# Attention and an expanded feed-forward stage in one kernel: the last rows stored tile by tile, zero fillers, pooled V summed on TensorE, weights split two chunks at a time, another order

## The chip, the cores and the metric

The kernel runs on one core of one Trainium2 chip. The metric is device time in microseconds (us), the median of several runs of one launch. The median before is 948.58 us over 3 runs (947.45 to 950.13).

## What is computed

q, k and v are float32, 8 batches x 8 heads x 576 positions x 64. Each head has a pooled attention (q, k and v averaged over groups of 4 positions, full softmax over 144 keys, result repeated 4 times) plus a local attention (keys at a distance below 4). The sum x, 4608 tokens x 512, passes through two matrix products with a rational function between them.

```
q_d, k_d, v_d = means over 4 positions
out_up  = repeat(softmax(q_d k_d^T / 8) v_d, 4)
out_loc = softmax(mask(q k^T / 8, |i - j| < 4)) v
x = (out_up + out_loc) as 4608 x 512
h = x @ w_in                                  # 512 -> 2048
g = (a0 + a1 h + a2 h^2 + a3 h^3) / (1 + |b0||h| + |b1| h^2 + 1e-6)
out = g @ w_out                               # 2048 -> 512
```

The weights come in as 64-bit words, which the kernel turns into float32 on the chip.

## The kernel before, in words

**Blocks and steps.** The tokens are nine blocks of 512: block b < 8 holds the first 512 positions of batch b, block 8 the last 64 positions (`REST`) of all eight batches. For each block 16 steps run, one for each 128 of the 2048 hidden features. A step has an h part (TensorE, `h_part`), a chain of six ScalarE and up to seven VectorE operations (`middle`) that leaves g as a high and a low part, gh and gl, and an o part (TensorE, `o_part`) that accumulates g @ w_out in four PSUM banks, one for each 128 tokens. Products are made of three terms: high by high, low by high, high by low. The 16 h parts of block 0 take whole float32 matmuls (L1073) instead. The last two steps of the last block are halved by tokens: the first covers tiles 0 and 1 for features 14 and 15, the second tiles 2 and 3.

**Attention** for a batch runs in four pairs of heads beside the steps of an earlier block. Batch 0 stands alone at the start; its four pairs are written in `first.0` to `first.3`, and its pooled V is summed over the four positions of a group by two loads and two accumulating GpSimd DMAs into `vf`, two tiles whose sum is made on TensorE: `part_b` in `weighted` (L899) multiplies the pooled weights with each of the two.

**Weights.** `weights` loads a chunk, scales it on ScalarE (L372) and rebuilds its bits on VectorE (L375, L378). `parts` takes the high part (ScalarE cast, L395) and the remainder as low part (VectorE, L398), chunk by chunk, 32 chunks.

**Stores.** `store` copies each finished PSUM bank (ScalarE L1244, or VectorE L1236 for odd tiles of the last block) and stores it: for blocks 0 to 7 one transfer of 128 rows of 2 KB each (L1248). A tile of the last block is 2 batches x 64 positions. There a pair of tiles is waited for, and two transfers of 64 rows x 2 tiles go out, one issued by SP (L1266), one by ScalarE (L1261).

**Order.** All operations are tasks with a cost in a planner (`Plan`), which lists them by urgency, and the table `SHIFT` moves single tasks in urgency. The engines then run in the fixed order that comes out. In the gaps that the planner sees on TensorE before step 0's o part, `warm` puts filler matmuls on the bf16 identity (L1423).

Of the kernel before, what the change touches and what calls it, by code (L numbers as in the profile page):

```python
# [208 lines left out]
def attention_moe(  # L209
# [107 lines left out]
    vf = [put(f"vf{i}", [KC, NPAIR, 2, 2, D], F32, low[0][half + 2 * i].at) for i in range(2)]  # L317
# [24 lines left out]

    add("POOL", 0.6, consts, (), (ident,))
# [13 lines left out]
    def weights(w, f, spot, due=None):  # L357
# [29 lines left out]
        if w and f >= WHOLE:  # L387
# [15 lines left out]


# [471 lines left out]
    def weighted(cs, bk, due):  # L876
# [128 lines left out]
        add("PE", 1.72 if len(cs) == 2 else 1.404, part_b, turn + pooled_v + ready, avb)  # L1005
# [221 lines left out]
    def store(k):  # L1227
        blk = blocks[k]
        due = due_h(blk.first + blk.nstep + 2)
        for sub in range(blk.nsub):  # L1230
# [20 lines left out]
            elif sub % 2:  # L1251
                both = flat(xsf[blk.slot][0].ap)[:, (sub - 1) * DM : (sub + 1) * DM]
                both = both.rearrange("p (b d) -> p b d", d=DM)
                whole = part(hi, None, 4 * (sub - 1) * DM, 8 * DM)
                rows = out.rearrange("(b s) d -> s b d", s=S)
                for i in range(2):
                    b = 2 * (sub - 1) + i
                    src, dst = both[i * REST : (i + 1) * REST], rows[FULL:, b : b + 3 : 2, :]
                    if i:
                        add(  # L1260
                            "ACT", 0.6, lambda src=src, dst=dst: nc.scalar.dma_start(out=dst, in_=src),  # L1261
                            (whole,), (), due=due + 2,
                        )
                    else:
                        add(
                            "SP", ISSUE, lambda src=src, dst=dst: nc.sync.dma_start(out=dst, in_=src),  # L1266
                            (whole,), (), due=due + 2, load=0.8,
                        )
# [10 lines left out]
    for r in range(POOL):  # L1279
        v = vf[r // 2]  # L1280
        if r % 2:
            add(
                "POOL", 0.93, lambda r=r, v=v: nc.gpsimd.dma_start(out=v.ap, in_=vp[0, r], accum_op=ALU.add),
                (v,), (v,), load=2.1, wait=6.4, more=0.0,
            )
        else:
            add("SP", ISSUE, lambda r=r, v=v: nc.sync.dma_start(out=v.ap, in_=vp[0, r]), (), (v,), load=1.7, more=2.1)
# [150 lines left out]
    with tc.manual_schedule(engines={getattr(ET, e) for e in ("PE", "DVE", "Activation", "Pool", "SP")}):  # L1438
# [24 lines left out]
WARM_FROM = 1.75  # L1463
# [20 lines left out]
H_WHOLE = 16  # L1484
POOL_COST = 4.2
# [19 lines left out]
    },  # L1505
# [4 lines left out]
    },  # L1510
# [4 lines left out]
    },  # L1515
# [4 lines left out]
    },  # L1520
# [8 lines left out]
    "load": {  # L1529
        0: -131.9, 2: 38.9, 3: -51.9, 4: -57.2, 5: -8.5, 6: -11.1, 7: -44, 8: -14.4, 9: -99.7, 10: -4.1,  # L1530
        11: -43.1, 12: 1, 13: -76.6,
    },
    "load.0": {
        0: 116.4, 1: 120.8, 2: 15.1, 3: -18.3, 4: 22.1, 5: -20.2, 6: -0.6, 7: -3.8, 8: 1.8, 9: 58.8,
        10: 77.9, 12: 2.9, 13: 11.4, 14: 4.1, 15: 26.4, 16: -32.6, 17: -22.1,
    },
    "load.1": {
        2: -8.9, 3: -0.7, 4: 0.3, 5: 4.8, 6: -32.4, 7: -3.1, 8: 70.8, 9: 10.4, 10: 46.9, 11: -111.9,
        12: 16.3, 13: -21.8, 14: 73.2, 15: -113.5, 16: -30.7, 17: 32.4,
    },  # L1540
    "local.0": {
        0: 23.6, 1: 8.5, 2: 279.5, 3: 745.1, 4: -58.8, 5: -79.6, 6: -80.6, 7: 111, 8: 6, 11: 3.9, 12: 156,
        13: 9.8, 14: 129.7,
    },
    "local.1": {
        0: -22.9, 1: 0.1, 2: 18.3, 3: 607, 4: -2, 5: 1.2, 7: 0.8, 8: -0.5, 9: 465.7, 10: -27.8, 11: -1.3,
        12: 71.5, 13: -5.5, 14: 278,
    },
    "mask": {0: -118.3, 1: -43.7},
    "middle.0": {  # L1550
        0: 10.7, 1: -34.3, 2: 205.9, 3: 4, 4: -0.2, 5: -0.8, 6: -3.4, 7: 91.2, 8: -738.2, 9: 46.5,
        10: 422.1, 11: 27.2, 12: -3.6,
    },
# [37 lines left out]
    "parts": {1: 122.9},  # L1591
# [144 lines left out]
```

## Time and profile before

| what | value |
|---|---|
| median of 3 runs | 948.58 us |
| the profiled execution's own time | 946.54 us |
| its span, first to last instruction | 944.8 us |
| PE (TensorE matmul) busy | 928.8 us, 98% |
| DVE (VectorE) busy | 873.3 us, 92% |
| ACT (ScalarE) busy | 773.6 us, 82% |
| POOL (GpSimd) busy | 148.5 us, 16% |
| instructions | 19636 |

Busy time counts filler matmuls too. The time outside the span is 946.54 - 944.8 = 1.74 us. PEld is TensorE's weight load, SPq and ACTq are the queues that issue transfers.

### The profile page before, as it was taken

To read this page: it belongs to the slowest core of one execution; us is meant where nothing else is said; L and a number is where in the kernel's file an instruction comes from. 1 tells how busy PE (TensorE), PEld (TensorE's weight loads), DVE (VectorE), ACT (ScalarE), POOL (GpSimd) and SP (SyncE) were. 2 spreads that over 40 slices of the span, in tenths; PEclk is the share of its full clock that TensorE was granted. 3 is DMA by queue.
4 is the path that set the end of the run, shared out by engine and by line. 5 is a ranking of instruction groups with operands and counts; after the bars stand their busy time and mean duration, and the time that the engine had idled before them with its cause. 6 is when DMAs were issued, how large, how long until landed. Compare 5 with 4: busy or idle time off the path is not lost.

```text
span 944.8 us, 19636 instructions
## 1 busy us (share of the span) xinstructions
PE 928.8 (98%) x7050; PEld 727.1 (77%) x7050; DVE 873.3 (92%) x1547; ACT 773.6 (82%) x1972; POOL 148.5 (16%) x176
## 2 busy tenths in 40 slices
PE   8999999999999999999999999999999999999996
PEld 7755666788787878787877878787878878887885
DVE  6999999999999999999999999999999988988886
ACT  4899999897897979796979798888988676767674
POOL 1042232130302122221212030304020000000000
PEclk9999999999999999999999999999999999999998
DMA  9697954544565646565657475656633010001001
GB/s 293 261 248 217 275 96 76 180 70 115 93 155 117 132 116 144 146 124 121 130 163 137 110 125 149 117 133 119 172 63 91 1 45 1 1 0 46 1 1 46
DMA packets 93098, 109.34 MB, mean 116 GB/s; under 512 B 23080, under 2 KB 75304, under 8 KB 93000
## 3 DMA queue, kind: packets, MB, share of 16 engines
q1 hardware_dynamic: 69480, 86.90, 30.7%
q0 software_dynamic: 23232, 20.66, 16.4%
q8 instruction: 56, 0.92, 0.4%
q10 hardware_dynamic: 288, 0.52, 0.2%
q14 instruction: 42, 0.34, 0.1%
HBM read 87.05 MB, written 20.99 MB: 114 GB/s over the span
## 4 chain that ended last, share of the span: by engine, by line
PE 60%; DVE 18%; ACT 16%; issue 4%; DMA 2%; DVEq 0%; SPq 0%; ACTq 0%
PE psum L1215 27%; PE psum L1085 26%; ACT m L1098 4%; DVE g L1177 4%; ACT el L625 3%; ACT gb L1098 3%; DVE m L1182 2%; DVE m L1142 2%; DVE m L1191 2%; PE psum L889 2%; DVE m L1147 2%; ACT ep L655 1%; DVE m L1151 1%; DVE xf L952 1%; DVE nm L590 1%
## 5 line engine op out<-in xcount | busy, mean ns | idle before, releaser
L1215 PE MATMUL psum<-wh,g 128*128 128x512 f32 x1152 | 369.9, 398 | 1.6 <-ACT xf L1244 0.9
L1085 PE MATMUL psum<-xs,wh 128*128 128x512 f32 (+1 forms) x1040 | 259.3, 389 | 0.4 <-ACT gb L1098 0.2
L1215 PEld LDWEIGHTS psum<-wh,g 128*128 128x128 f32 x1152 | 213.4, 188 | 58.1 <-DVE g L1177 6.8
L1098 ACT ACTIVATE m<-psum,cf 128x512 f32<-128x512 f32 x288 | 210.7, 739 | 55.3 <-PE psum L1085 43.6
L1085 PEld LDWEIGHTS psum<-xs,wh 128*128 128x128 f32 x1040 | 191.9, 188 | 43.0 <-ACT gb L1098 3.0
L1215 PE MATMUL psum<-wl,g 128*128 128x512 f32 x576 | 224.3, 390 | 0.0
L1177 DVE TENSOR_TENSOR g<-m,m 128x512 fp32r<-128x512 f32 x288 | 194.7, 685 | 30.4 <-ACT m L1098 22.4
L1085 PE MATMUL psum<-xs,wl 128*128 128x512 f32 (+1 forms) x520 | 138.8, 389 | 0.0
L1098 ACT ACTIVATE gb<-m 128x512 f32<-128x512 f32 x144 | 92.0, 639 | 45.4 <-DVE m L1142 39.5
L1215 PEld LDWEIGHTS psum<-wl,g 128*128 128x128 f32 x576 | 108.2, 188 | 21.7
L1098 ACT ACTIVATE gb<-psum,cf 128x512 f32<-128x512 f32 x144 | 113.7, 790 | 5.8 <-PE psum L1215 5.6
L1085 PEld LDWEIGHTS psum<-xs,wl 128*128 128x128 f32 x520 | 96.1, 188 | 20.1
L1142 DVE SCALAR_TENSOR_TENSOR m<-m,cf,m 128x512 f32<-128x512 f32 x144 | 106.8, 742 | 1.9 <-ACT m L1098 1.7
L1151 DVE TENSOR_TENSOR m<-m,gb 128x512 f32<-128x512 f32 x144 | 98.4, 684 | 7.7 <-ACT gb L1098 6.6
L1098 ACT ACTIVATE m<-gb 128x512 f32<-128x512 f32 x144 | 91.7, 637 | 15.2 <-DVE m L1147 14.0
L442 POOL DMA_DIRECT2D vq<-in_vq_dram x60 | 52.4, 944 | 315.1 <-DMA vq<-in_vq_dram 287.4
L1182 DVE SCALAR_TENSOR_TENSOR m<-m,g 128x512 f32<-128x512 f32 x144 | 98.6, 685 | 2.4
L1191 DVE TENSOR_TENSOR m<-m,m 128x512 f32<-128x512 f32 x144 | 98.8, 686 | 1.8
L442 POOL DMA_DIRECT2D pq<-in_qkp_dram x84 | 73.1, 906 | 165.6 <-DMA pq<-in_qkp_dram 150.3
L1147 DVE TENSOR_TENSOR m<-m,m 128x512 f32<-128x512 f32 x144 | 98.1, 682 | 0.3 <-ACT m L1098 0.3
L1098 ACT ACTIVATE m<-psum 128x512 f32<-128x512 f32 x144 | 86.5, 601 | 2.7 <-DVE g L1177 1.8
L625 ACT ACTIVATE el<-el,nm 128x64 f32<-128x64 f32 x240 | 80.8, 353 | 2.3 <-DVE nm L617 2.0
(100 smaller groups left out, 882.8 us busy)
## 6 DMA issues: line engine op xcount, KB each, us to landing
qk<-in_qk_dram SPq DMA_DIRECT2D x32, 590.0 KB, 6.0
pq<-in_qkp_dram POOLq DMA_DIRECT2D x84, 144.0 KB, 3.6
vw<-in_vw_dram SPq DMA_DIRECT2D x32, 320.0 KB, 10.9
out_dram<-xf SPq DMA_DIRECT2D x34, 256.0 KB, 2.4
bounce<-tt SPq DMA_DIRECT2D x96, 80.0 KB, 1.9
eu<-bounce SPq DMA_DIRECT2D x40, 160.0 KB
sl<-in_w_out_dram SPq DMA_DIRECT2D x12, 512.0 KB, 4.3
vq<-in_vq_dram POOLq DMA_DIRECT2D x60, 96.0 KB, 3.6
```

The lines of the kernel that those rows point to most:

```text
L442: lambda d=dst, x=src, r=r: nc.gpsimd.dma_start(out=d.ap, in_=rows(x, r), accum_op=ALU.add),
L625: nc.scalar.activation(out=s.el.ap[:, k, j, :], in_=view[:, j, k, :], func=AF.Exp, bias=nm[:, 5 * j + k : 5 * j + k + 1], scale=scale, acc ...
L889: nc.tensor.matmul(dst, lhsT=c.slot.vw.ap[m : m + D, w, :], rhs=src, start=True, stop=True, skip_group_check=True,)
L1085: nc.tensor.matmul(ph.ap[:, f * t : (f + 1) * t], lhsT=(high, low)[j][0][fc].ap[:, c, :], rhs=blk.x[i].ap[:, c, t0 : t0 + t], start=(part_ ...
L1098: add("ACT", cost, lambda: nc.scalar.activation(out=out_.ap, in_=in_, func=func, **kw), (room_in, cf, *more), (out_,))
L1142: lambda: v.scalar_tensor_tensor(out=tb.ap, in0=tq.ap, scalar=b1, in1=tb.ap, op0=ALU.mult, op1=ALU.add),
L1147: add("DVE", 0.602, lambda: v.tensor_tensor(out=ta.ap, in0=ta.ap, in1=tq.ap, op=ALU.mult), (ta, tq), (ta,))
L1151: add("DVE", 0.602, lambda: v.tensor_tensor(out=ta.ap, in0=ta.ap, in1=u.ap, op=ALU.add), (ta, u), (ta,))
L1177: return v.tensor_tensor(out=out, in0=x, in1=y, op=ALU.mult)
L1182: lambda: v.scalar_tensor_tensor(out=tb.ap, in0=tb.ap, scalar=CONE, in1=gh.ap.bitcast(F32), op0=ALU.add, op1=ALU.mult),
L1191: add("DVE", 0.602, lambda: v.tensor_tensor(out=ta.ap, in0=ta.ap, in1=tb.ap, op=op), (ta, tb), (ta,))
L1215: nc.tensor.matmul(ob[sub].ap, lhsT=g[i].ap[:, g0 : g0 + P], rhs=flat((high, low)[j][1][fc].ap), start=(fc == 0 and m == 0), stop=(fc == N ...
```

## The change

Six things change. The tiles of the last block leave one by one: each is stored from its 128 partitions by one SP transfer whose DRAM side is written as 2 batches x 64 rows x 512. The fillers read a tile of zeros, made by VectorE, in place of the identity, and may start at 1.0 us of the planner's time. Pooled V of batch 0 stays in four tiles, loaded by four SP transfers, and `part_b` makes four terms for each half of the keys. The parts of w_in are taken two chunks at a time, and those of w_out too from chunk 2 on. The table `SHIFT` is replaced, and with it the order on all engines.

```diff
@@ the tiles of the parts @@
-            for f in range(NFC):
-                t = put(f"{name}{w}_{f}", [P, NCC, P], F32R)
...
+            for f in range(0, NFC, 2):
+                t = put(f"{name}{w}_{f}", [P, 2, NCC, P], F32R)
...
-    vf = [put(f"vf{i}", [KC, NPAIR, 2, 2, D], F32, low[0][half + 2 * i].at) for i in range(2)]
+    vf = [put(f"vf{i}", [KC, NPAIR, 2, 2, D], F32, low[0][half + 2 * i].at) for i in range(POOL)]
...
+    plain = put("plain", [P, P], BF16, high[0][0].at)
+    add("DVE", 0.06, lambda: nc.vector.memset(plain.ap, 0.0), (), (plain,), due=-100.0)
@@ parts @@
+        if f >= SINGLE[w]:
+            if f % 2:
+                both_parts(w, f - 1, due)
+            return
...
+    def both_parts(w, f, due):
+        hi, lo, word = (x[w][f // 2] for x in sides)
+        src = word.ap.bitcast(F32)
+        add("ACT", 0.88, lambda: nc.scalar.copy(out=hi.ap, in_=src), (lo,), (hi,), due=due)
+        add(
+            "DVE", 1.133,
+            lambda: nc.vector.tensor_tensor(out=lo.ap, in0=src, in1=hi.ap.bitcast(F32), op=ALU.subtract),
+            (lo, hi), (lo,), due=due,
+        )
@@ weighted @@
-        add("PE", 1.72 if len(cs) == 2 else 1.404, part_b, turn + pooled_v + ready, avb)
+        add("PE", 1.72 if len(cs) == 2 else 2.36, part_b, turn + pooled_v + ready, avb)
@@ store, last block @@
-            elif sub % 2:
-                both = flat(xsf[blk.slot][0].ap)[:, (sub - 1) * DM : (sub + 1) * DM]
-                both = both.rearrange("p (b d) -> p b d", d=DM)
...
-                rows = out.rearrange("(b s) d -> s b d", s=S)
-                for i in range(2):
-                    b = 2 * (sub - 1) + i
-                    src, dst = both[i * REST : (i + 1) * REST], rows[FULL:, b : b + 3 : 2, :]
...
+            else:
+                dst = bass.AP(
+                    tensor=out.tensor, offset=out.offset + (2 * sub * S + FULL) * DM,
+                    ap=[[S * DM, 2], [DM, REST], [1, DM]],
+                )
+                add(
+                    "SP", ISSUE, lambda osb=osb, dst=dst: nc.sync.dma_start(out=dst, in_=osb),
+                    (room,), (), due=due + 2, load=0.8,
+                )
@@ pooled V of batch 0 @@
-    for r in range(POOL):
-        v = vf[r // 2]
-        if r % 2:
-            add(
-                "POOL", 0.93, lambda r=r, v=v: nc.gpsimd.dma_start(out=v.ap, in_=vp[0, r], accum_op=ALU.add),
...
+    for r, v in enumerate(vf):
+        add("SP", ISSUE, lambda r=r, v=v: nc.sync.dma_start(out=v.ap, in_=vp[0, r]), (), (v,), load=1.5)
@@ fillers @@
-                banks[7].ap[:, FULL - P :], lhsT=identb.ap, rhs=identb.ap,
+                banks[7].ap[:, FULL - P :], lhsT=plain.ap, rhs=plain.ap,
...
-WARM_FROM = 1.75
+WARM_FROM = 1.0
+SINGLE = (0, 2)
...
-    "alone.0": {0: -77.2, 2: 1.5, 3: -118.1, 4: -6.9},
+    "alone.0": {0: -64.9, 1: -24.7, 3: -21.5, 4: -80},
```

The order at three places. First SP's queue at its end, before; the tiles of the last block lie in xf_0 side by side, and the shape is that of the DRAM side:

```order
L745 DMA bounce_p<-tp_201 32x5x80
L745 DMA bounce<-tt_193 32x4x160
L745 DMA eq_200<-bounce_p 64x3x144 x2
L745 DMA eu_198<-bounce 64x2x320 x2
L1248 DMA out_dram<-xf_0_154 128x512 x4
L1248 DMA out_dram<-xf_0_158 128x512 x4
L1266 DMA out_dram<-xf_0_154 64x2x512 x2
```

and in the change:

```order
L766 DMA bounce_p<-tp_153 32x5x64
L766 DMA eu_150<-bounce 64x2x320 x2
L766 DMA eq_152<-bounce_p 64x3x144
L1269 DMA out_dram<-xf_0_106 128x512 x4
L1269 DMA out_dram<-xf_0_110 128x512 x4
L1278 DMA out_dram<-xf_0_106 2x64x512 x4
```

Two transfers of 64x2x512 on SP (and the two like them at the end of ACT's queue) become four of 2x64x512, all on SP.

Second, PE's last rows, before; g_168 and g_170 are gh and gl of the first half step (tiles 0 and 1), g_167 and g_169 those of the second (tiles 2 and 3), wh and wl the parts of w_out:

```order
L1215 MATMUL psum<-wl_15_150,g_168 128x512
L1215 MATMUL psum<-wh_14_86,g_167 128x512 x2
L1215 MATMUL psum<-wh_15_87,g_167 128x512 x2
L1215 MATMUL psum<-wl_14_148,g_167 128x512 x2
L1215 MATMUL psum<-wl_15_150,g_167 128x512 x2
L1215 MATMUL psum<-wh_14_86,g_170 128x512 x2
L1215 MATMUL psum<-wh_15_87,g_170 128x512 x2
L1215 MATMUL psum<-wh_14_86,g_169 128x512
L1215 MATMUL psum<-wh_15_87,g_169 128x512
L1215 MATMUL psum<-wh_14_86,g_169 128x512
L1215 MATMUL psum<-wh_15_87,g_169 128x512
```

and in the change, where one tile holds two chunks of weights, g_120 and g_122 are gh and gl of the first half step, g_119 and g_121 those of the second:

```order
L1236 MATMUL psum<-wl_14_102,g_120 128x512
L1236 MATMUL psum<-wh_14_71,g_120 128x512
L1236 MATMUL psum<-wl_14_102,g_120 128x512
L1236 MATMUL psum<-wh_14_71,g_122 128x512 x4
L1236 MATMUL psum<-wh_14_71,g_119 128x512 x4
L1236 MATMUL psum<-wl_14_102,g_119 128x512 x4
L1236 MATMUL psum<-wh_14_71,g_121 128x512 x4
```

The four matmuls on gl of the first half step, which finish tiles 0 and 1, have moved ahead of the second half step's twelve.

Third, PE in batch 0's attention, from where the second pair's part_b begins, before (ept: pooled weights, et: local weights, vf and vw: values):

```order
L710 MATMUL psum<-ident,el_222 128x128 x4
L899 MATMUL psum<-ept_206,vf_239 64x144 x2
L899 MATMUL psum<-ept_206,vf_240 64x144 x2
L899 MATMUL psum<-ept_206,vf_239 64x144 x2
L899 MATMUL psum<-ept_206,vf_240 64x144 x2
L889 MATMUL psum<-et_208,vw_205 64x58 x2
L889 MATMUL psum<-et_208,vw_205 64x54 x2
L889 MATMUL psum<-et_208,vw_205 64x58 x16
```

and in the change:

```order
L731 MATMUL psum<-ident,el_174 128x128 x4
L920 MATMUL psum<-ept_158,vf_191 64x144 x2
L920 MATMUL psum<-ept_158,vf_192 64x144 x2
L920 MATMUL psum<-ept_158,vf_193 64x144 x2
L920 MATMUL psum<-ept_158,vf_194 64x144 x2
L920 MATMUL psum<-ept_158,vf_191 64x144 x2
L920 MATMUL psum<-ept_158,vf_192 64x144 x2
L920 MATMUL psum<-ept_158,vf_193 64x144 x2
L920 MATMUL psum<-ept_158,vf_194 64x144 x2
L910 MATMUL psum<-et_160,vw_157 64x58 x2
L910 MATMUL psum<-et_160,vw_157 64x54 x2
L582 MATMUL psum<-pq_181 64x144 x6
```

Eight matmuls on pooled V become sixteen for each pair. Over the whole attention of batch 0 the fillers fall from 170 to 131.

## Rows read from the trace of the kernel before

**Rows 1.** The page, part 1: engine, busy us (share of the span), instructions.
```profile
PE 928.8 (98%) x7050; PEld 727.1 (77%) x7050; DVE 873.3 (92%) x1547; ACT 773.6 (82%) x1972; POOL 148.5 (16%) x176
```
**Rows 2.** Busy time by stretch: length, then busy us by engine, granted clock, DMA share, GB/s.
```profile
20.00:30.00 10.00, 9.43 (x177) 8.15 (x175) 7.27 (x20) 9.73 (x47) 0.00 (x0) 1.00 1.03 375
...
80.00:90.00 10.00, 8.40 (x38) 5.36 (x37) 10.00 (x21) 10.00 (x28) 3.30 (x4) 1.00 0.94 267
...
500.00:600.00 100.00, 99.79 (x805) 79.82 (x804) 95.80 (x172) 84.85 (x233) 20.95 (x24) 1.00 0.59 131
...
900.00:945.00 45.00, 37.60 (x187) 31.30 (x185) 32.73 (x51) 24.89 (x40) 0.00 (x0) 0.94 0.08 24
```
**Rows 3.** The chain that ended last, 880 to 945 us: start us, length us, what.
```profile
907.90 2.72 PE psum L1215 x12
...
933.92 4.00 PE psum L1215 x16
```
**Rows 4.** Timeline of the end, by engine: start us, length us, instruction, count.
```profile
935.87 2.03 PE L1215 MATMUL psum<-wh,g 128*128 128x512 f32 x8
936.75 1.31 ACT L1244 COPY xf<-psum 128x512 f32<-128x512 f32 x2 [3.61 <-PE psum L1215]
937.75 1.59 ACTq L1261 DMA_DIRECT2D out_dram<-xf  x2
937.94 0.69 DVE L1236 COPY xf<-psum 128x512 f32<-128x512 f32 x1 [0.27 <-PE psum L1215]
```
**Rows 5.** Transfers, 937 to 945 us: busy tenths in 40 slices; queue: packets, MB, share.
```profile
DMA  0000000000298998989999989998451000000000
...
q10 hardware_dynamic: 288, 0.52, 24.2%
q1 hardware_dynamic: 288, 0.52, 20.6%
```
**Rows 6.** Transfers, 860.5 to 863 us, one store alone.
```profile
GB/s 0 0 0 0 0 0 0 0 0 0 0 0 0 0 0 0 0 0 197 229 360 426 426 360 393 393 426 295 393 230 66 0 0 0 0 0 0 0 0 0
DMA packets 144, 0.26 MB, mean 105 GB/s; under 512 B 16, under 2 KB 16, under 8 KB 144
...
q1 hardware_dynamic: 144, 0.26, 27.9%
```
**Rows 7.** Transfers, 132 to 135 us, two loads of pooled V, 72 rows each.
```profile
q1 hardware_dynamic: 168, 0.15, 17.2%
...
vp<-in_vp_dram SPq DMA_DIRECT2D x2, 72.0 KB
```
**Rows 8.** Groups by line and shape: count, busy us, mean ns, idle before.
```profile
L899 PE MATMUL psum<-ept,vf 72*64 72x144 f32 x64 | 5.0, 294 | 0.0
L1423 PE MATMUL psum<-identb 128*128 128x128 bf16 x170 | 12.3, 235 | 1.6 <-DVE identb L346 1.6
L398 DVE TENSOR_TENSOR wl<-wb,wh 128x512 fp32r<-128x512 f32 x32 | 21.4, 676 | 0.0
L395 ACT CAST wh<-wb 128x512 fp32r<-128x512 f32 x32 | 19.8, 653 | 0.0
L731 ACT COPY et<-psum 128x128 f32<-128x128 f32 x4 | 1.1, 270 | 0.0
```
**Rows 9.** Timeline of PE, 28 to 56 us.
```profile
33.24 1.20 PE L899 MATMUL psum<-ept,vf 72*64 72x144 f32 x16
34.37 1.38 PE L889 MATMUL psum<-et,vw 64*64 64x58 f32 x40
...
43.25 12.28 PE L1073 MATMUL psum<-xf,wb 128*128 128x512 f32 x28
```
**Rows 10.** ACT's exponentials of the last pair, 28 to 32 us.
```profile
L625 ACT ACTIVATE el<-psum,nm 128x64 f32<-128x64 f32 x10 | 3.0, 318 | 0.2 <-DVE nm L617 0.2
```
**Rows 11.** PE's waits, 43 to 165 us: total us, times, longest.
```profile
PE psum L1073 <- ACT gb L1098: 2.0, 2, 1.6
PE psum L528 <- ACT el L625: 1.4, 1, 1.4
```

More of the change, by code (lines that the diff above doesn't have):

```diff
@@ L256, in flat @@
         return t.rearrange("p a b -> p (a b)")
-    high, low, bits = [], [], [[], []]
+    high, low, bits = ([[], []] for _ in range(3))
+    sides = {id(x): [[], []] for x in (high, low, bits)}
     for name, parts in (("wh", high), ("wl", low)):
         for w in range(2):
-            parts.append([])
-            for f in range(NFC):
-                t = put(f"{name}{w}_{f}", [P, NCC, P], F32R)
-                parts[w].append(t)
+            for f in range(0, NFC, 2):
+                t = put(f"{name}{w}_{f}", [P, 2, NCC, P], F32R)
+                both = [(parts, t)]
                 if parts is low:
-                    bits[w].append(put(f"wb{w}_{f}", [P, NCC, P], I32, t.at))
+                    both.append((bits, put(f"wb{w}_{f}", [P, 2, NCC, P], I32, t.at)))
+                for to, x in both:
+                    sides[id(to)][w].append(x)
+                    for i in range(2):
+                        to[w].append(part(x, x.ap[:, i], i * 4 * NCC * P, 4 * NCC * P))
+    sides = [sides[id(x)] for x in (high, low, bits)]
     xs, xsf = [], []
@@ L386, in weights @@
         add("DVE", 0.6, lower, (spot, lo), (lo,))
-        if w and f >= WHOLE:
+        if w:
             parts(w, f)
     def parts(w, f, due=None):
+        if f >= SINGLE[w]:
+            if f % 2:
+                both_parts(w, f - 1, due)
+            return
         hi, lo, word = high[w][f], low[w][f], bits[w][f]
@@ L1250, in store @@
                 )
-            elif sub % 2:
-                both = flat(xsf[blk.slot][0].ap)[:, (sub - 1) * DM : (sub + 1) * DM]
-                both = both.rearrange("p (b d) -> p b d", d=DM)
-                whole = part(hi, None, 4 * (sub - 1) * DM, 8 * DM)
-                rows = out.rearrange("(b s) d -> s b d", s=S)
-                for i in range(2):
-                    b = 2 * (sub - 1) + i
-                    src, dst = both[i * REST : (i + 1) * REST], rows[FULL:, b : b + 3 : 2, :]
-                    if i:
-                        add(
[L1261 to L1268, printed above, removed]
+            else:
[7 more added lines that the diff above has]
+                )
     order = sorted(((w, f) for w in range(2) for f in range(NFC)), key=lambda c: c[1] / 2 + 1.5 * c[0])
@@ L1278, in attention_moe @@
         load_qk(c)
-    for r in range(POOL):
-        v = vf[r // 2]
-        if r % 2:
-            add(
-                "POOL", 0.93, lambda r=r, v=v: nc.gpsimd.dma_start(out=v.ap, in_=vp[0, r], accum_op=ALU.add),
[L1284 to L1287, printed above, removed]
+    for r, v in enumerate(vf):
+        add("SP", ISSUE, lambda r=r, v=v: nc.sync.dma_start(out=v.ap, in_=vp[0, r]), (), (v,), load=1.5)
     for c in c0:
@@ L1536 @@
     },
     "load.1": {
-        2: -8.9, 3: -0.7, 4: 0.3, 5: 4.8, 6: -32.4, 7: -3.1, 8: 70.8, 9: 10.4, 10: 46.9, 11: -111.9,
-        12: 16.3, 13: -21.8, 14: 73.2, 15: -113.5, 16: -30.7, 17: 32.4,
+        0: 198.5, 1: 7.7, 2: 5.9, 3: -1.4, 4: 109.9, 6: 19.3, 7: -46.6, 8: 18.4, 9: -9.6, 11: -8.4, 12: 4.8,
+        13: -4.9, 14: 18.4, 16: -10.1, 17: -15.3,
     },
     "local.0": {
-        0: 23.6, 1: 8.5, 2: 279.5, 3: 745.1, 4: -58.8, 5: -79.6, 6: -80.6, 7: 111, 8: 6, 11: 3.9, 12: 156,
-        13: 9.8, 14: 129.7,
+        0: -46.2, 2: 874.5, 3: 1185.3, 4: -32.4, 5: -29.9, 6: -61.3, 7: 42.5, 8: 6.2, 10: 113.1, 11: 7.3,
@@ L1544 @@
+        12: 25.5, 13: 10.6, 14: 180.1,
     },
     "local.1": {
-        0: -22.9, 1: 0.1, 2: 18.3, 3: 607, 4: -2, 5: 1.2, 7: 0.8, 8: -0.5, 9: 465.7, 10: -27.8, 11: -1.3,
-        12: 71.5, 13: -5.5, 14: 278,
+        0: -59, 1: 22.8, 2: 461.6, 3: 651.1, 4: 4.1, 5: -44.7, 6: 1.6, 7: 96.9, 8: -20.6, 9: 317.9, 10: 17,
+        11: 8.9, 13: 57, 14: 172.8,
     },
-    "mask": {0: -118.3, 1: -43.7},
+    "mask": {0: -10.8, 1: 69.9},
     "middle.0": {
-        0: 10.7, 1: -34.3, 2: 205.9, 3: 4, 4: -0.2, 5: -0.8, 6: -3.4, 7: 91.2, 8: -738.2, 9: 46.5,
-        10: 422.1, 11: 27.2, 12: -3.6,
+        0: -3.5, 1: -128, 2: 64.4, 4: -18.9, 5: -40.1, 6: 31.7, 8: -1089.9, 9: -52.9, 10: 74.4, 11: -28.2,
+        12: -118.9,
@@ L1560 @@
+        12: -15.8,
     },
     "middle.3": {
-        0: 7.5, 1: -124.4, 2: -0.7, 3: -24.3, 4: -281.9, 5: 348.1, 6: 1.3, 7: 81.7, 8: 59.2, 9: -89.8,
-        10: -75.7, 11: 1.4, 12: 130,
+        0: -189.2, 1: -235.8, 3: -30.3, 4: -181.3, 6: -36, 7: -13, 8: 72.1, 9: -180.5, 10: 82.3, 11: -8.8,
+        12: 36.4,
     },
     "middle.4": {
-        0: -5.2, 1: 297.3, 2: 16.9, 4: -278.5, 5: -4.9, 6: -7.6, 7: -32.6, 8: -68, 9: 61.8, 10: -8.9,
-        11: -17.9, 12: -2.1,
+        0: -85.9, 1: -20.4, 2: -7.3, 3: -183.1, 4: -134, 5: 451.6, 7: -44.3, 8: -169.3, 9: 18.9, 10: 1.8,
@@ L1568 @@
+        11: -84.2, 12: 250.5,
     },
     "middle.5": {
-        0: -1.6, 1: -12.8, 2: 31.8, 3: -115.2, 4: -2.7, 5: 2.1, 6: 20, 7: -142.6, 8: 78.1, 9: -14.7,
-        10: -28.9, 11: -1.8, 12: 356.5,
+        0: 78.8, 1: 9.1, 2: 8.2, 3: -156.4, 4: -118.7, 5: 267.8, 6: -22.9, 7: -85.4, 8: 130, 10: 0.2,
+        11: 2.7, 12: 3.1,
     },
     "middle.6": {
-        0: 33.8, 1: -0.2, 2: 123.1, 3: 307.2, 4: 123.1, 5: -48, 6: -56, 7: -18.3, 8: 261.3, 9: -10.2,
-        11: 108.9, 12: 565.7,
+        0: 3.8, 1: -25, 2: 16.2, 3: 368.3, 4: 4.5, 5: -66.9, 6: -61.4, 7: -10.6, 8: 401.5, 9: 8.8,
@@ L1576 @@
+        11: 201.6, 12: 539,
     },
     "middle.7": {
-        0: 191.4, 1: 167.4, 2: 16.9, 3: 286.5, 4: -27.9, 5: 274.9, 6: 599.9, 8: -1.6, 9: -19.9, 10: 76.4,
-        11: 306.3, 12: 206.3,
-    },
[10 rows of a table removed]
-    "parts": {1: 122.9},
[10 rows of a table removed]
+        0: 393.6, 1: 156.6, 2: 87.8, 3: 605.3, 4: 19.5, 5: 429.2, 6: 807.8, 7: 9.9, 8: 48.6, 9: -46.7,
+        10: 183.8, 11: 287.9, 12: 169.5,
+    },
[10 rows of a table added]
+    "parts": {0: 4.1, 1: 227.2},
[9 rows of a table added]
     },
     "quad.1.1": {
[7 rows of a table removed]
[6 rows of a table added]
     },
     "quad.2.0": {
[8 rows of a table removed]
[8 rows of a table added]
     },
     "quad.2.1": {
[7 rows of a table removed]
-    },
@@ L1644 @@
     },
     "turned.1": {
[3 rows of a table removed]
-    },
[10 rows of a table removed]
+        0: 48.8, 1: 304.6, 2: 21.7, 3: 36.9, 4: -10.5, 5: -71.5, 6: 32.1, 7: 128.3, 8: -15.9, 10: 38.4,
+        12: 53.2, 13: -41.9, 14: -1.7, 15: 33.2, 16: 14.5, 18: 56.6, 20: -3.3, 21: 585.1, 22: 8.3, 26: 1,
+        27: -7.9,
+    },
[10 rows of a table added]
 }
```

19 lines of the change are left out of this document (9 added, 10 removed), and 162 rows, old and new, of the table SHIFT.

## The prediction

> **What bounds the kernel now.** I read first the share of each engine over the span, then the busy time stretch by stretch, then the chain that ended last, and at the two ends of the kernel the timeline and the transfers. TensorE is busy 98% of the span [rows 1]. By stretches the reader sees three parts. In the long middle TensorE has hardly a gap: 99.79 of 100 us between 500 and 600 [rows 2]. The number of its matmuls there doesn't change, so a new order can take away a few tenths of a us at most. In the first 160 us it does wait, 8.40 of 10 us busy at the worst [rows 2]. At the end only 37.60 of the last 45 us are busy [rows 2]: the last matmul ends at 935.87 + 2.03 = 937.90 [rows 4], and 944.8 - 937.9 = 6.9 us of the span remain for two copies and the stores. The chain at the end is TensorE's alone, 2.72 us for 12 matmuls, 0.227 us each, until the last 16, which begin late [rows 3]. So three things can move the total: when TensorE's dense run begins, the stalls up to 160 us, and the tail. The sum is made against the profiled execution, whose own 946.54 us lie 2.04 below the median of the three runs, 948.58; I add the differences to the median. A measurement of this kernel can tell about 0.3%, 2.85 us, from no change.
>
> **The tail, which decides.** Before, the four stores go out together. The transfer engines are busy from about 938.8 to 943.3 [rows 5], 1.1 us after the first issue at 937.75 [rows 4], and the span ends 1.5 us after the last byte. One store of 256 KB on its own leaves 144 packets, of which 16 are under 512 B [rows 6]: 128 rows of 2 KB, and 16 small ones. I read the small ones as one for each of the 16 engines used. Two of the last stores (64 rows outermost, 2 tiles inside) leave 288 packets on each queue, 256 of data and again 16 each [rows 5]. Two loads of pooled V, 72 rows outermost, leave 168, that is 144 and only 12 each [rows 7]. So a transfer isn't always dealt over 16 engines: 128 and 64 rows give 16, 72 rows give 12, each time the largest number up to 16 that divides the outermost count. In all of these both sides have the same outermost count. The new store doesn't: 128 partitions on one side, 2 batches x 64 rows on the other. Either the smaller side decides and two engines carry everything, or the SBUF side does and sixteen do. I take two, as a transfer has to be cut at the same places on both sides.
>
> By the Trainium skill, DMA: Bandwidth & Descriptors, section "Why a DMA increments its semaphore by 16 and not by 1", the number of engines is the largest up to 16 that divides the slowest dimension of both patterns; the trace agrees for 72 rows, and no run here shows two sides that differ. By that rule the stores take what I work out next for two engines; by the rows alone both readings below stand.
>
> The price: one store keeps 27.9% of 16 engines busy for 2.5 us [rows 6], 11.2 engine-us, and on two engines that is 5.6 us. If all four use the same two, 22.3 us. Bounds: at the best rate seen, 426 GB/s over 16 engines [rows 6], two move 53 GB/s, and 1.05 MB take 19.7 us. At what the four stores cost when they ran together, (24.2 + 20.6)% of 16 engines over 8 us = 57.3 engine-us [rows 5], they take 28.7 us. I take 22.3, since two engines press on memory no more than the lone store did.
>
> The start of the stores moves ahead. The four matmuls that finish tiles 0 and 1 now stand before the last twelve; tile 0's last one has 13 behind it, so its copy can begin 13 x 0.227 = 2.95 us before TensorE's end, takes 1.31 / 2 = 0.66 [rows 4], and its bytes flow about 1.1 us after the issue: 1.2 us before TensorE's end, where they now begin 0.9 after it. Then 22.3 us and the 1.5 us at the close: 22.6 us behind TensorE's end instead of 6.9, **+15.7 us** (+13.1 to +22.1 by the bounds). SP's queue holds nothing else there, so issuing costs nothing; ScalarE loses two issues that no one waited behind.
>
> TensorE's own end stays. VectorE's copy of tile 1, 0.69 us, now stands ahead of the last two operations on gl, which the last four matmuls wait for. That can cost some 0.4 us, about what is saved from the late start of the last 16 matmuls, which took 4.00 us where 16 x 0.227 = 3.63 would do [rows 3]. Net nothing.
>
> **The start.** Pooled V as four terms doubles the 64 matmul records of L899 [rows 8]. One pair's 16 step on in 34.37 - 33.24 = 1.13 us [rows 9], so +4.5 us of TensorE work for four pairs. The 39 fillers fewer are 39 x 12.3 / 170 = 2.8 us less [rows 8], but a filler lies in a gap and its loss brings nothing forward. From the second pair's part_b at 33.24 to the run of step matmuls at 43.25 [rows 9] TensorE is nearly full, so three pairs' terms, +3.4 us, lie on the path there unless that stretch begins earlier. It can: the order lets ScalarE make the second pair's transposed weights ahead of the last pair's ten exponentials, 3.0 us [rows 10]. I take +0.4 for the start, between -1 (the chain through ScalarE gives more than it costs) and +3.4. Without the two accumulating GpSimd transfers the first pair is ready no later, but nothing waits for the first pair. Four loads in place of two on SP stand among weight loads, 576 KB more ahead of some of them; what covers that is that the first step's matmuls can't run before all four pairs are done.
>
> **Weights by two chunks.** 17 instructions stand for 32 on ScalarE (0.653 us each) and on VectorE (0.676) [rows 8]. 512 columns take 0.653 and 128 take 0.270 [rows 8], so 0.14 us of each is fixed, and 15 x 0.14 = 2.1 us fall away on ScalarE; I take the same for VectorE, as an estimate. The bounds are nothing and 15 whole instructions. Both engines are full at 80 to 90 us [rows 2], and TensorE waited 2.0 + 1.4 us for ScalarE until 165 us [rows 11], so a gain can be had, up to 3.4 us; but a chunk is then ready only with its partner. I take -0.4. Fillers on zeros and their earlier start: the granted clock is 1.00 at 20 to 30 us [rows 2] and the step matmuls keep TensorE dense from 43 us, so nothing.
>
> **Sum**: 15.7 + 0.4 - 0.4 = +15.7. The profiled execution comes to 962.2, the median to **964.3 us**.
>
> **The rivals.** (1) *The SBUF side decides and sixteen engines carry each store.* For it: the 128 rows are on the side that TensorE's results lie in, and the trace has no pair of unequal sides. Against it: the 12 of 72. Then the last tile's copy ends 0.73 us behind TensorE's end [rows 4], its bytes begin 1.1 later, take 0.83 (13 slices of 2.5 / 40 us) [rows 6], and 1.5 us close: 4.2 in place of 6.9, so 945.9 us. That isn't slower; with the start's and the stalls' -1 and -3.4 it is faster, with the start's +3.4 it is the same. The point from which it decides: eight engines or more for a store. The Trainium skill, DMA: Bandwidth & Descriptors, "Rules for kernel authors", advises one 128-partition transfer in place of two over halves, which taken alone speaks for this rival; no run here compares the two. (2) *The start costs what its terms cost*: +3.4 in place of 0.4, with two engines 967.3. For it: the nearly full 10 us before 43.25. Against it: the exponentials moved behind. (3) *The clock falls in the start*, with 39 fillers fewer and their operands zero. The dense 10 us before 43.25 would at worst take 20: 974. Against it: the granted clock was 1.00, its 2.4 GHz level, at 20 to 30 us and at 80 to 90 us, gaps of 1.6 us among them [rows 2, 11]. (4) *The new order brings nothing that can be seen*: this is in the forecast already, as the middle has no gap to give.
>
> **How the numbers follow.** Two engines, the forecast: 0.83; of that (2) has 0.2. Rival (1): 0.13, half of it faster by over 0.3%, half within. Rival (3): 0.02. Otherwise: 0.02. Slower by over 0.3%: 0.83 + 0.02 + 0.01 = 0.86; within 0.06; faster 0.08. The range goes from the fastest price of the stores with the stalls gone, 948.58 + 13.1 - 3.4 = 958.3, to the dearest with the dearer start, 948.58 + 22.1 + 3.4 = 974.1. It leaves out rival (1) and some 0.05 more.
>
> **What would show it.** Right: after the last matmul some 22 us in which only the transfer queue of SP works, at about 50 GB/s and a share of transfer engines near 2/16; 520 packets or so for the last four stores, 8 of them small (two for each store) if two engines are used. Wrong: 16 small packets for each store and an end 4 to 5 us after TensorE's. The start is right if the first long run of step matmuls begins at 42 to 47 us; the weights by two if an instruction on 1024 columns takes about 1.17 us on ScalarE. The forecast as a whole is wrong if the tail behind the last matmul is under 15 us.

## The result, and the profile after

The changed kernel takes **960.94 us** (median of 6 runs, 958.73 to 964.63) against 949.06 for the kernel before on the same chip (6 runs, 947.45 to 951.38): a ratio of 1.0128, 95% interval 1.0101 to 1.0154. That is slower, by 11.9 us. The forecast was 964.3, with 958.3 to 974.1 around it. The profiled execution took 959.22 us; its span is 957.4, 12.6 more than the 944.8 before. Three executions in the experiments below, of 1147.92, 2350.43 and 5228.38 us, were slow as a whole, and no ratio counts them.

Busy time of the engines first, the page's part 1 after the change (it answers to [rows 1]).

```profile
PE 928.6 (97%) x7075; PEld 728.7 (76%) x7075; DVE 872.7 (91%) x1533; ACT 771.8 (81%) x1957; POOL 147.7 (15%) x174
```

TensorE has as much work as before, 928.6 against 928.8 us. So the 12.6 us are time in which it stands still. Busy time by stretch tells where (after; the columns are those of [rows 2]).

```profile
40.00:100.00 60.00, 56.35 (x374) 33.14 (x372) 57.34 (x106) 54.66 (x138) 15.85 (x18) 1.00 0.83 239
...
60.00:70.00 10.00, 7.87 (x70) 5.31 (x69) 8.98 (x16) 8.34 (x22) 5.90 (x7) 1.00 0.83 225
100.00:120.00 20.00, 20.00 (x230) 12.94 (x229) 20.00 (x38) 20.00 (x64) 6.19 (x7) 1.00 0.82 239
500.00:600.00 100.00, 99.98 (x808) 80.38 (x807) 96.21 (x175) 85.42 (x236) 20.78 (x25) 1.00 0.60 133
100.00:930.00 830.00, 829.87 (x6061) 661.53 (x6060) 778.40 (x1355) 687.74 (x1714) 131.16 (x151) 1.00 0.43 99
900.00:945.00 45.00, 35.73 (x178) 29.62 (x176) 31.95 (x48) 23.47 (x38) 0.00 (x0) 0.95 0.03 11
```

Four of these stretches of the kernel before, which its rows above don't have:

```profile
40.00:100.00 60.00, 58.02 (x430) 34.73 (x429) 59.83 (x118) 58.34 (x150) 15.84 (x18) 1.00 0.86 238
...
60.00:70.00 10.00, 9.98 (x116) 6.50 (x117) 10.00 (x19) 9.76 (x33) 6.80 (x8) 1.00 0.88 157
100.00:120.00 20.00, 18.59 (x167) 12.09 (x166) 18.93 (x38) 18.76 (x66) 5.09 (x6) 1.00 0.94 284
100.00:930.00 830.00, 826.46 (x5978) 657.21 (x5977) 776.76 (x1359) 685.05 (x1717) 130.12 (x150) 1.00 0.44 100
```

From 100 to 930 us TensorE stood 3.54 us before and 0.13 now, a gain of 3.4, of which 20.00 - 18.59 = 1.4 lies between 100 and 120 us. From 40 to 100 us it is the other way round, 3.65 us of standing in place of 1.98, most of it at 60 to 70. The rest of the story is the tail. The timeline of the end, after:

```profile
932.57 0.57 ACT L1265 COPY xf<-psum 128x512 f32<-128x512 f32 x1
933.16 9.61 SPq L1278 DMA_DIRECT2D out_dram<-xf  x4
934.14 0.68 DVE L1257 COPY xf<-psum 128x512 f32<-128x512 f32 x1
936.29 1.15 PE L1236 MATMUL psum<-wh,g 128*128 128x512 f32 x4 [0.64 <-DVE g L1198]
937.03 0.59 ACT L1265 COPY xf<-psum 128x512 f32<-128x512 f32 x1 [3.89 <-PE psum L1236]
937.48 0.69 DVE L1257 COPY xf<-psum 128x512 f32<-128x512 f32 x1 [1.33 <-PE psum L1236]
```

The last matmul ends at 936.29 + 1.15 = 937.44 (before 937.90 [rows 4]). 957.4 - 937.44 = 20.0 us of the span remain behind it, where 6.9 remained. What fills them is in the transfers from 930 to 958 us (slices of 0.7 us):

```profile
DMA  0000001011111111111111111111111111111000
GB/s 0 0 0 0 0 0 23 29 23 35 44 50 53 53 50 50 53 53 47 53 53 53 47 53 53 50 50 53 53 50 50 53 53 50 50 53 53 12 0 0
DMA packets 520, 1.05 MB, mean 37 GB/s; under 512 B 8, under 2 KB 8, under 8 KB 520
...
q1 hardware_dynamic: 520, 1.05, 10.2%
```

and in two stretches of the same time:

```profile
934.20:936.30 2.10, 1.46 (x8) 0.91 (x6) 1.91 (x4) 0.00 (x0) 0.00 (x0) 1.00 0.12 25
...
940.00:950.00 10.00, 0.00 (x0) 0.00 (x0) 0.00 (x0) 0.00 (x0) 0.00 (x0) 0.51 0.13 51
```

Bytes flow from about 934.2 to 956, 21.8 us, at 23 to 44 GB/s in the first 3.5 us and at 47 to 53 behind them; before, the four stores were through in 4.5 us [rows 5]. The 8 small packets are two for each store, where a store of 128 rows had 16 [rows 6], and the transfer engines' share is 0.13, two of 16 (0.125): two engines carry everything.

### The profile page after: what moved, and what is told of

Same layout as the page of the kernel before. It is cut to its first block, busy times and chain, and to the rows that moved or that the text cites. A ratio compares the mean times of both kernels' runs of the same rounds, so it can differ in the third digit from the quotient of the medians.

```text
span 957.4 us, 19630 instructions
## 1 busy us (share of the span) xinstructions
PE 928.6 (97%) x7075; PEld 728.7 (76%) x7075; DVE 872.7 (91%) x1533; ACT 771.8 (81%) x1957; POOL 147.7 (15%) x174
## 4 chain that ended last, share of the span: by engine, by line
PE 86%; DVE 5%; DMA 3%; ACT 3%; issue 1%; SPq 0%; DVEq 0%; ACTq 0%
PE psum L1236 39%; PE psum L1106 35%; PE psum L1094 4%; DMA st<-in_w_in_dram 2%; PE psum L910 2%; PE psum L502 1%; PE psum L582 1%; DVE g L1198 1%; ACT m L1119 1%; PE psum L948 1%; PE psum L920 1%; DVE m L1163 1%; ACT gb L1119 1%; DMA sl<-in_w_in_dram 1%; ACT el L646 1%
```

## The experiments

The times before in these runs lie at 946.85, 947.05 and 947.21 us, so each version is compared by its ratio to the kernel before, measured beside it. The ratio is taken over all runs of both; that of the two medians can differ from it by up to 0.0008, or 0.8 us. In the cuts of the edits, `...` stands for lines left out.

**Only the change's store undone.** Does the rest of the change cost anything?

```diff
-                dst = bass.AP(tensor=out.tensor, offset=..., ap=[[S * DM, 2], [DM, REST], [1, DM]])
...
+            elif sub % 2:
...
+                rows = out.rearrange("(b s) d -> s b d", s=S)
+                src, dst = both[i * REST : (i + 1) * REST], rows[FULL:, b : b + 3 : 2, :]
```

> The change with only its last store put back (four transfers of 64x2x512, two on SP and two on ACT, each behind both tiles of its pair); the orders of VectorE, GpSimd and TensorE stay as in the change but for one neighbouring pair of matmuls. Theory (the store is the whole loss, the rest of the change is worth half a us): TensorE's last matmul ends at about 937.4 and the tail is 6.9 us again, so a span near 944.3 and a median near 948.5 us, between 0.5 below and 0.5 above before. Rival (the start or the clock carries part of the loss): 951 us or more. Rival (the new order brought the 3.4 us that it saved between 100 and 900 us, and its losses at 40 to 100 us and at the end belong to the store's order): 946 us or less.

Measured: 947.08 us (12 runs), ratio 0.9996, 0.9978 to 1.0014. The transfers of the end, 930 to 945 us, have their 64 small packets back:

```profile
DMA packets 576, 1.05 MB, mean 70 GB/s; under 512 B 64, under 2 KB 64, under 8 KB 576
```

The whole loss is the store's. All the rest together, the new order with it, comes to nothing that can be told. The rival by which the gain of 3.4 us should show falls too: the profile of this version has the gain (829.79 of 830 us busy from 100 to 930) and the loss of 60 to 70 us (8.03 of 10). Its tail is 5.6 us, not the 6.9 expected, as the new order finishes the first pair of tiles earlier and that pair leaves at 935.7. TensorE's end, 937.13 + 1.16 = 938.3, is 0.9 us later than expected; 0.7 of that is standing in the first 100 us that the change doesn't have.

**The store alone, in the kernel before.** Same queues, same places in every order, same bytes. On the DRAM side the outermost index is the batch (2) in place of the row (64); with it, each transfer takes one tile from 128 partitions in place of two tiles from 64.

```diff
-                rows = out.rearrange("(b s) d -> s b d", s=S)
+                rows = out.rearrange("(b s) d -> b s d", s=S)
...
-                    src, dst = both[i * REST : (i + 1) * REST], rows[FULL:, b : b + 3 : 2, :]
+                    src, dst = both[:, i * DM : (i + 1) * DM], rows[b : b + 2, FULL:, :]
```

> The kernel before with nothing changed but the index that is outermost in its last four stores: 2x64x512 (one tile each) in place of 64x2x512, on the same queues, two on SP and two on ACT, at the same places of every engine's order. Theory (the smaller outermost count sets the number of engines, the same two for both queues): the bytes begin at about 938.8, take the 21.8 us that they took in the change, and 1.5 us close: a span of 962.1, 17.3 us longer, near 966.3 us; 8 small packets among 520, some 50 GB/s. Rival (each queue has engines of its own, so that two pairs of engines share the bytes): 938.8 + 10.9 + 1.5 = 951.2, near 955.5 us. Rival (one queue that issues four transfers behind each other is what is slow, not the shape): as before, 949 us.

Measured: 964.28 us (4 runs), ratio 1.0179, 1.0149 to 1.0208; span 962.3 where 962.1 was expected. The transfers, 930 to 965 us:

```profile
DMA packets 521, 1.06 MB, mean 30 GB/s; under 512 B 8, under 2 KB 8, under 8 KB 520
...
q1 hardware_dynamic: 260, 0.52, 4.4%
q10 hardware_dynamic: 260, 0.52, 3.8%
```

Writing the batch outermost costs 17.4 us by itself (964.28 - 946.85). The stores of the change start earlier, tile by tile; that gives part of it back, 12.5 us being left by the two ratios, (1.0128 - 0.9996) x 949.

**Two queues.** Here the stores of the change alternate between SP and ACT.

```diff
+                if sub % 2:
+                    add("ACT", 0.6, lambda osb=osb, dst=dst: nc.scalar.dma_start(out=dst, in_=osb), ...)
```

> The change with the stores of tiles 1 and 3 issued by ACT and those of tiles 0 and 2 by SP, all still 2x64x512. Theory (the same two engines serve both queues): no change, 960 to 961 us, 50 GB/s in all. Rival (another queue uses another two engines): two tiles on each pair of engines, tile 1's bytes from 936.0 and tile 3's behind them to 946.8, a span of 948.3 and about 951.8 us, at 100 GB/s.

Measured: 962.29 us (4 runs), ratio 1.0157, 1.0125 to 1.0188, with 49 to 52 GB/s in all once the first 2.6 us are over, and 8 small packets. Ten us of it:

```profile
940.00:950.00 10.00, 0.16 (x1) 0.00 (x0) 0.69 (x1) 0.33 (x1) 0.00 (x0) 0.66 0.13 51
```

The share is 0.13 as with one queue, so two engines are at work and not four: the same two serve both queues, and one queue's issuing isn't what is slow.

**Halves.** Each tile goes out as two transfers of 64 rows, so that both sides have 64 outermost.

```diff
-                    ap=[[S * DM, 2], [DM, REST], [1, DM]],
...
+                    for i in range(2):
...
+                            ap=[[DM, REST], [1, DM]],
...
+                        nc.sync.dma_start(out=dst, in_=osb[i * REST : (i + 1) * REST])
```

> The change with each tile's store as two transfers of 64 rows, both on SP at the place of the one, so that both sides have 64 rows outermost; all other orders word for word those of the change. Theory (outermost count): 16 small packets for each transfer, 128 in all, the last tile's copy ends at 938.2, issue and first byte 1.1 us, the bytes under 1 us, 1.5 us to close: a span near 941.7, near 945.2 us, 15.7 us below the change. Rival (one SP queue with stores behind each other is the bound): still near 960 us. Rival (64 partitions reach only half of the engines): a tail of some 6 us, near 947 us.

Measured: 946.57 us (12 runs), ratio 0.9989, 0.9976 to 1.0002, which is 13.2 us below the change by the two ratios, (1.0128 - 0.9989) x 949; 15.7 had been expected. The transfers, 930 to 965 us:

```profile
DMA packets 640, 1.05 MB, mean 30 GB/s; under 512 B 128, under 2 KB 128, under 8 KB 640
```

16 small ones for each of the 8 transfers: sixteen engines again. The tail was 5.5 us in the profile, 1.3 more than expected: the last two tiles follow each other on SP as four issues, and their bytes flow at only some 200 GB/s. TensorE's end lay at 939.1 in that profile, 1.7 us later than in the change, where the same 7075 matmuls were busy 930.7 us in place of 928.6: a dip of the granted clock, which the last section gives. Leaving tile by tile isn't worth measurably more than leaving by pairs (0.9989 against 0.9996, the intervals overlap).

**62 and 2 rows.** Is it the disagreement of the two sides, or the number?

```diff
-                    for i in range(2):
+                    for i, r, n in ((0, 0, 62), (0, 62, 2), (1, 0, 62), (1, 62, 2)):
```

> The halves version with each transfer of 64 rows cut into one of 62 rows and one of 2. Theory (the number of engines is the largest up to 16 that divides the outermost count): 62 rows go to two engines, as in the change, though both sides agree: some 4 small packets for a pair of cuts, 32 in all, 50 GB/s, about 22 us of bytes, near 961 us. Rival (only the two sides' disagreement, or a count under 16, keeps a transfer from sixteen engines): 62 rows spread over about sixteen, at most 2 us more than the halves version, under 949 us.

Measured: 960.76 us (one run). The transfers, 930 to 960 us:

```profile
DMA packets 544, 1.05 MB, mean 35 GB/s; under 512 B 32, under 2 KB 32, under 8 KB 544
```

544 - 32 = 512 rows and 32 small packets, two for each of 16 transfers. Both sides agree on 62 rows, and still two engines carry them, since 2 is the largest number up to 16 that divides 62. So the number decides, as with the 72 rows of [rows 7].

**Both queues, and tile 1 copied by ScalarE.** What hangs on VectorE at the very end?

```diff
-            if k == len(blocks) - 1 and sub % 2:
+            if k == len(blocks) - 1 and sub == 3:
...
+                    if i:
+                        add("ACT", 0.6, lambda src=src, dst=dst: nc.scalar.dma_start(out=dst, in_=src), ...)
```

> The halves version (two transfers of 64 rows for each tile) with two things more: of each tile's two transfers one goes out on SP and one on ACT, and tile 1 is copied by ScalarE, so that VectorE's copy of 0.68 us no longer stands ahead of the last gl; VectorE's and TensorE's order is otherwise that of the change but for one neighbouring pair of matmuls. Theory (TensorE's last stalls hang on VectorE's chain to gl, and the last two tiles' four issues on SP pass the bytes on at only 200 GB/s): the last matmul ends 0.65 us earlier than with that copy (a last stall of 0.64 gone or the one before it shorter), the last bytes leave 0.7 us sooner, 1.3 us in all: near 945.2 us. Rival (the stall hangs on ScalarE, or the four transfers' bytes are the bound): 946.6 us, as the halves version.

Measured: 946.18 us (11 runs), ratio 0.9985, 0.9976 to 0.9995. TensorE's last two stalls, in this version's timeline:

```profile
934.01 1.21 PE L1236 MATMUL psum<-wh,g 128*128 128x512 f32 x4 [0.93 <-DVE g L1198]
...
936.35 1.17 PE L1236 MATMUL psum<-wh,g 128*128 128x512 f32 x4 [0.20 <-DVE g L1198]
```

In the halves version they are

```profile
935.22 1.20 PE L1236 MATMUL psum<-wh,g 128*128 128x512 f32 x4 [1.09 <-DVE g L1198]
...
937.96 1.16 PE L1236 MATMUL psum<-wh,g 128*128 128x512 f32 x4 [0.64 <-DVE g L1198]
```

so the copy cost 1.73 - 1.13 = 0.60 us there, and the tail behind the last matmul is 942.4 - 937.5 = 4.9 in place of 5.5 us. In the profiles the expected 1.3 us are nearly there (0.60 + 0.6). The ratios differ by 0.0004 alone, which is inside their intervals, so the medians don't show them. This version is faster than the kernel before by 0.15%, under the 0.3% of the prediction's bound though its interval leaves out 1, and faster than the change by 1.4%.

**Two of the four terms of pooled V.** The halves version with half of the sum left out of TensorE's work.

```diff
-                terms = [(v, kc) for kc in range(2) for v in vp_of(c)]
+                terms = [(v, kc) for kc in range(2) for v in vp_of(c)[:2]]
```

> The halves version with two of the four terms of pooled V of batch 0 left out of TensorE's work (half of that sum is missing; the four loads stay): TensorE issues 16 matmuls fewer in each pair's record group, 1.05 us a pair, 4.2 us in all. Theory (what the terms cost at the start is mostly hidden, because the waits for ScalarE at 52 to 72 us come next): the first long run of step matmuls begins 1 to 3 us earlier, the waits between 50 and 75 us grow by nearly as much, and the time falls by under 1 us: near 946.0. Rival (the start costs what its terms cost, rival 2 of the prediction): three pairs' terms, 3.2 us, reach the end: 943.4 us.

Measured: 944.91 us (12 runs), ratio 0.9972, 0.9960 to 0.9985: 1.6 us below the halves version (0.0017 x 947), between the two expectations (946.0 and 943.4). The two intervals overlap, so the runs don't decide between them. Its profiled execution, 946.05 us, doesn't show the start at its best. Busy time of 2 us stretches there:

```profile
20.00:22.00 2.00, 0.66 (x12) 0.49 (x9) 1.99 (x5) 2.00 (x16) 0.00 (x0) 1.00 0.99 232
22.00:24.00 2.00, 1.51 (x38) 1.48 (x39) 1.66 (x5) 2.00 (x14) 0.00 (x0) 0.94 1.04 301
24.00:26.00 2.00, 2.00 (x19) 1.80 (x18) 1.90 (x6) 2.00 (x8) 0.00 (x0) 0.50 1.01 382
26.00:28.00 2.00, 2.00 (x21) 1.49 (x20) 0.61 (x1) 0.03 (x1) 0.00 (x0) 0.50 1.03 392
28.00:30.00 2.00, 2.00 (x15) 1.97 (x14) 1.56 (x5) 1.29 (x4) 0.00 (x0) 0.50 1.00 376
```

TensorE did 0.66 and then 1.51 us of work in 2, and from 24 to 30 us the granted clock was 0.50, its level of 1.2 GHz. A second profile of this version, that of the execution of 2350.43 us, can't be compared with the others: its long run begins at 79.5 us.

**Fewer bytes ahead of the values.** The same with a quarter of the third and fourth loads.

```diff
-        add("SP", ISSUE, lambda r=r, v=v: nc.sync.dma_start(out=v.ap, in_=vp[0, r]), (), (v,), load=1.5)
...
+            out=v.ap[:, :1] if r > 1 else v.ap, in_=vp[0, r][:, :1] if r > 1 else vp[0, r],
```

> The version with two terms, in which the third and fourth loads of pooled V, which no matmul reads any more, bring a quarter of their columns (72x256 in place of 72x1024): 432 KB less on SP's queue ahead of the values and the weights, every order as it was. Theory (the loads that moved from GpSimd to SP delay what TensorE waits for at 18 to 26 us, values L910 and pooled V L920, and those waits, in some executions with a fall of the granted clock behind them, are part of what the start costs): the waits for these transfers shrink from 1.4 to 2.3 us to under 0.7, and the time falls by 0.5 to 1.5 us against the version with all loads, to 0.9960 of before. Rival (the transfer engines are full until 34 us whatever stands first, and the later waits for ScalarE take the gain back): 0.9972 of before, as with all loads.

Measured: 943.53 us, ratio 0.9961, 0.9946 to 0.9975 (six of its seven runs lie at 942.73 to 943.77, where the version with all loads spread from 942.74 to 947.34). TensorE's timeline, around the start of the long run:

```profile
21.00 1.14 PE L910 MATMUL psum<-et,vw 64*64 64x58 f32 x32 [0.59 <-DMA vw<-in_vw_dram]
...
42.30 8.85 PE L1094 MATMUL psum<-xf,wb 128*128 128x512 f32 x20
52.20 1.98 PE L1094 MATMUL psum<-xf,wb 128*128 128x512 f32 x4 [1.05 <-ACT gb L1119]
54.60 3.70 PE L1094 MATMUL psum<-xf,wb 128*128 128x512 f32 x8 [0.42 <-ACT m L1119]
```

The wait for pooled V is gone and that for the values is 0.59, against 0.9 for values and 0.5 for pooled V in the change. The halves version's profile, with all four loads, shows neither of these two waits, so they come in some executions only. The time lies where the theory put it, but the interval holds the rival (0.9972) too: that the loads cost some 1 us isn't shown. The long run begins at 42.30, 2.3 us ahead of the halves version (44.60), and the waits for ScalarE from 40 to 100 us add up to 4.5 us (2.7 + 1.4 + 0.4) where they were 3.5 (2.2 + 0.9 + 0.4): about 1 of the 2.3 us goes back there.

**Fillers on the identity again**, in the halves version.

```diff
-                banks[7].ap[:, FULL - P :], lhsT=plain.ap, rhs=plain.ap,
+                banks[7].ap[:, FULL - P :], lhsT=identb.ap, rhs=identb.ap,
```

> The halves version with the fillers' operands set back to the identity in place of the tile of zeros; number, places and order of the fillers stay. Theory (the fillers' values cost and bring nothing): within 0.2% of the halves version, near 946.6 us, granted clock 1.00 from 10 to 60 us. Rival (zeros let the granted clock fall later, at 64 to 72 us, where the halves version's profile shows 0.82 and 0.75): the dip of 1.7 us is gone in the profile and in the time, 944.9 us.

Measured: 946.58 us (10 runs), ratio 0.9997, 0.9986 to 1.0007; the halves version has 946.57. The zeros bring nothing that can be told, and the rival's 944.9 is out. The dip doesn't follow the operands: where 1.00 was expected from 10 to 60 us, this version's profile shows a granted clock of 0.50 from 26 to 30 us, behind waits of 0.8 and 1.5 us for the values and for pooled V, and 1.00 at 60 to 80 us.

## Why the prediction held, and where it was off

**Direction and mechanism: right.** Two engines carried the stores; 520 packets, 8 of them small, some 50 GB/s, a share of 0.13, one queue at work. Of SP's four issues one took 4.5 us, but the bytes flowed on meanwhile, so issuing cost nothing, as forecast. Rival (1), that the SBUF side decides, is out: it would have given 945.9 (945.8, as 13 slices of 2.5 / 40 us are 0.81 and not 0.83), and 62 rows against 62 show that the number on the smaller side, with its divisors, decides.

By the Trainium skill, DMA: Bandwidth & Descriptors, section "Why a DMA increments its semaphore by 16 and not by 1", the engines of a transfer are the largest number up to 16 that divides the slowest dimension of both patterns; the runs agree, for two sides that differ (128 and 2: two engines) and for 62. The Trainium skill, DMA: Bandwidth & Descriptors, section "Rules for kernel authors", advises one transfer of 128 partitions in place of two over halves; here the halves took 946.57 us and the one 960.94, as the halves have 64 outermost on both sides and the one has 2 on one of them.

**The tail: right but 2.6 us too long** (+15.7 by the sum; 20.0 - 6.9 = +13.1 in the profile).
- The price of the bytes nearly held: 22.3 us forecast from one lone store [rows 6], 21.8 measured.
- The start of the stores was the term that was off. The prediction let tile 0's bytes flow 1.2 us before TensorE's end, from 13 matmuls of 0.227 us behind tile 0's last. They flowed 937.44 - 934.2 = 3.2 us before it. Two stalls, 1.08 and 0.64 us, stand among those 13 matmuls, so that TensorE's end lay further behind tile 0 than its work alone puts it; they are 1.7 of the 2.0 us.

**TensorE's last stalls: "net nothing" was 1.4 us.** They add up to 1.72 us, where 0.3 stood before. "Some 0.4" for VectorE's copy ahead of the last gl measured 0.60 (halves version against both queues, in their profiles), and the late start that was to be saved stayed: without the copy 1.13 us are left. The end of TensorE's work now hangs on VectorE, as the chain that ended last shows (after):

```profile
934.14 0.68 DVE xf L1257
934.82 0.61 DVE m L1212
935.45 0.70 DVE g L1198
936.16 0.14 issue
936.29 1.17 PE psum L1236 x4
```

**The middle: wrong.** "A few tenths at most" was read from 500 to 600 us [rows 2], where TensorE had 0.21 us to give. From 100 to 930 us it had 3.54, and 3.41 of them went. Of these, 1.41 lay at 100 to 120 us, among the stalls up to 160 us that the prediction did name; the other 2.0 lay behind 160 us, where one dense stretch had stood for 770 us that weren't all like it. Whether the order or the weights by two took them no run separates; the store didn't, as the version with the old store has them too.

**The start and the stalls behind it: both had the wrong size.** The long run of step matmuls begins at 44.58 in place of 43.25 [rows 9], 1.3 us later and inside the 42 to 47 that were given. Half of the terms taken out brings 1.6 us with overlapping intervals, which settles neither +0.4 nor rival (2)'s +3.4. For the stalls up to 160 us the prediction took a gain of 0.4. TensorE stood 1.98 us from 40 to 100 and 1.41 from 100 to 120 before, and 3.65 and nothing after: a loss of 0.3, as the waits from 40 to 100 us, for ScalarE's gb above all, grew by 1.7. "Nothing waits for the first pair" was wrong too. TensorE's waits after, from 10 to 40 us and then from 40 to 100 us (total us, times, longest):

```profile
PE psum L910 <- DMA vw<-in_vw_dram: 0.9, 1, 0.9
PE psum L920 <- DMA vf<-in_vp_dram: 0.5, 1, 0.5
...
PE psum L1094 <- ACT gb L1119: 1.6, 1, 1.6
PE psum L549 <- ACT gb L1119: 1.3, 1, 1.3
```

The first two, for the first pair's values and pooled V, had no counterpart before. They cost little on balance: TensorE stood 3.3 us in the first 40 us before and after. Those first us also hold the worst stretch of the start, 7.73 of 10 us busy before, and not the 8.40 that the prediction called the worst.

**Weights by two: a little more per instruction, an open worth in the end.** The groups after:

```profile
L422 DVE TENSOR_TENSOR wl<-wb,wh 128x1024 fp32r<-128x1024 f32 x15 | 18.2, 1213 | 0.0
L419 ACT CAST wh<-wb 128x1024 fp32r<-128x1024 f32 x15 | 16.2, 1099 | 0.0
```

Against two of 653 and 676 ns [rows 8] an instruction of ScalarE saves 0.21 us and one of VectorE 0.14, where 0.14 was said of both. Whether any of it reached the end by itself wasn't tried: undoing it moves the planner's whole order.

**The sum.** Gains of 3.4 (100 to 930 us) and of 0.2 (less busy time), and losses of 1.7 (40 to 100 us) and 1.4 (the last stalls), leave TensorE's end 0.5 us earlier; the store adds 13.1 behind it. That is 12.6 in the profile, 11.9 in the medians. That TensorE's end hardly moved, as forecast, is luck: the prediction had none of these four at its size, and they cancel. The stores' price, which decides, isn't luck. Rival (3), the clock, didn't decide: the granted clock of the profile after is 1.00 from 0 to 930 us. Yet it isn't nothing, as the last section tells.

## What to carry to other kernels

Before a store or load is written in another shape, look at the outermost count of both sides: 128 partitions on one side are worth nothing if the other begins with 2, and a count like 62 is as bad as 2. The number of small packets of a lone transfer tells at a glance how many engines carried it. And a claim that "the middle has nothing to give" needs the idle time of the whole middle, not of its densest 100 us.

## What was not expected of the hardware

- Short stalls in the first 70 us are in some executions followed by a lower granted clock. In the profile of the halves version TensorE worked 1.80 of the 4 us from 64 to 68, and the granted clock was 0.82 in these and 0.75 in the next 4 us. In the profile of the version with two terms it was 0.50 from 24 to 30 us, and its long run began at 45.80, against 42.30 with fewer bytes and no dip. The same gaps don't always bring it: with the stores on two queues TensorE did nothing at all from 20 to 22 us, and the granted clock stayed at 1.00. The executions of one kernel spread with it: with identity fillers, 948.98 and 949.13 us at a mean clock of 0.994 and 0.995, and 945.43 to 946.93 in the other eight, at 0.996 to 0.999.
- A second queue doesn't bring a second pair of engines: four stores on SP and ACT by turns moved 49 to 52 GB/s in all at a share of 0.13, as on SP alone.
- On two engines the first us went slower than the rest: in the change 25 GB/s from 934.2 to 936.3 us and 51 from 940 to 950, at nearly the same share (0.12 and 0.13). No run shows why.
